# Gated mix of a long convolution and an MLP: the convolution by halves of 1024, three spectral products per frequency, the sums on POOL

## The chip, the core and the metric

The kernel runs on one core of one Trainium2 chip. The core has TensorE (PE in the profile; PEld is its weight load), VectorE (DVE), ScalarE (ACT), GpSimd (POOL) and SyncE (SP, which here only issues DMAs). The metric is the device time of one execution in microseconds (us).

## What is computed

The inputs are q, k, v and x = q of shape (1, 2048, 512), short and long convolution kernels per channel, and the two weights of an MLP of width 1792.

```python
x = A_q
g = sigmoid((x * gate_w).sum(-1, keepdims=True))
# a: short causal convolution of k (4 taps), times v, then a causal convolution of
#    length 2048 with ssm_k per channel (by FFT of 4096), plus kv * ssm_D, times q
kv = k_shift * v
y = irfft(rfft(kv, 4096) * rfft(ssm_k, 4096))[:2048] + kv * ssm_D
a = q * y
b = relu(x @ w1) @ w2
out = g * a + (1 - g) * b
```

All of it is float32. The kernel adds ssm_D to the first tap of ssm_k, so that the second term of y needs no work of its own.

## The kernel before

Two streams of work share the engines. The MLP has 4 chunks of 512 tokens and 14 slices of the hidden width. To keep float32 accuracy, each operand is split into a high and a low part (`parted`, `relu`, `rest`), and each product is three matmuls of 128x128 by 128x512: lines L314 to L316 for the first layer, L341 to L343 for the second, 1344 matmuls in all. ACT makes the high part of the hidden layer (hh, L326) and DVE the low part (hl, L329).

The long convolution is a Fourier transform written as small matmuls in float32, each of which PE runs as two passes. It works in three stages, with DRAM tensors `sa` and `sb` between them for the transposes:

- Stage one (`conv_h`, `conv_x`, `stage1`): for each of 8 pieces c, the long kernel (h) and the product kv (x, made by DVE from four taps, L432 to L448) are multiplied by a 64x128 matrix of complex exponentials (L380). Four matmuls of 64 rows by 128 columns fill four PSUM banks; ACT copies them out (L386) and SP stores them to `sa`.
- Stage two (`conv_mid`): for each of 8 groups g, the second transform of h and of x (`rounds`, L476: eight tiles of 64x32 per round, two rounds each), the complex product of both spectra on ACT and DVE (copies L490 and L493, eight products L506, four sums L513), and the first inverse transform (`inverse`, L524: 16 tiles of 32x64 in two rounds), copied out by ACT and DVE (L533, L535) and stored to `sb`.
- Stage three (`conv_end`): for each pair of 16 token blocks, the last transform (L586, four matmuls of 128x64), then the gate, the product with q (L595) and the sum with the MLP's result (L548). The MLP's result of the first 12 blocks waits in the DRAM tensor `bd` (L353, L599).

The kernel issues nothing in program order. Every operation is given to a planner (`Plan.add`) with an engine, a planned duration, a rank, what it depends on, and what it takes and gives of the buffers in `room` ("cv" are four of the eight PSUM banks; the other four hold the second layer's sums). `Plan.order` steps through time with these planned durations and writes down a fixed order for each engine; on the chip each engine runs that order and waits on semaphores where data or buffers aren't there. So the order on every engine is fixed beforehand, and bursts of small tiles (`tiles=True`) stand between runs of MLP matmuls. All loads and stores go through SP's queue, except two small constants that POOL loads.

Of the kernel before, what the change touches and what calls it, by code (L numbers as in the profile page):

```python
# [18 lines left out]


# [5 lines left out]
def _w(e):  # L26
    return np.exp(-2j * np.pi * (np.asarray(e) % (4 * S)) / (4 * S))
# [13 lines left out]
def _constants():  # L41

    n1, k1 = np.arange(64)[:, None], np.arange(64)[None]
    w = _w((4 * k1 + 1) * 32 * n1)
    s1 = np.stack([w.real, w.imag], -1).reshape(64, 128)
    s1 = np.concatenate([s1, s1], 0)

    fw = np.zeros((2, 2, 32, NJ, 2, 32))  # L50
    iv = np.zeros((4, 32, 8, 2, 2, 2, 32))
    n2, k2 = np.arange(32)[:, None], np.arange(32)[None]
    for j in range(NJ):
        for b in range(2):
            k1 = 2 * j + b
            c = _w((4 * k1 + 1 + 256 * k2) * n2)
            fw[b, 0, :, j, 0] = c.real
            fw[b, 1, :, j, 0] = -c.imag
            fw[b, 0, :, j, 1] = c.imag
            fw[b, 1, :, j, 1] = c.real  # L60
            c = np.conj(c.T)
            iv[j % 4, :, j // 4, 0, b, 0] = c.real
            iv[j % 4, :, j // 4, 1, b, 0] = -c.imag
            iv[j % 4, :, j // 4, 0, b, 1] = c.imag
            iv[j % 4, :, j // 4, 1, b, 1] = c.real
    cc = np.concatenate([fw.reshape(P, 8, 2 * P), iv.reshape(P, 8, 2 * P)], 2)


    c = np.conj(_w((4 * np.arange(64)[:, None] + 1) * 32 * np.arange(64)[None])) / S
    ib = np.stack([c.real, -c.imag], 1).reshape(P, 64)  # L70
    return s1, cc, ib
# [7 lines left out]
class Plan:  # L79
# [19 lines left out]
    def order(self):  # L99
# [14 lines left out]
        while True:  # L114
            for eng, ops in ready.items():
# [4 lines left out]
                if eng == "PE" and any(o["rank"][0] == 1 and not o["take"] for o in ops):  # L120
                    held = {t for o in ops + soon if o["rank"][0] == 0 and len(o["take"]) > 1 for t in o["take"]}
# [83 lines left out]
def build(tc, wf, xp, qn, kn, vn, hn, dn, sh, gw, w1, w2, cs1, ccc, cib, out):  # L205
# [11 lines left out]
    sa = dram.tile([2, P, 32, D], F32, name="sa")  # L217
    sb = dram.tile([P, 32, D], F32, name="sb")
# [3 lines left out]
            "cc": 2, "acc": ACC, "tmp": TMP, "ev": EV, "r": RB, "ha": HAB, "p": PB, "bv": BVB,  # L222
# [151 lines left out]
    def stage1(t, c, key, rank, after, give):  # L374
        def go():
            for r in range(R):
                z = slice(r * D, (r + 1) * D)
                for half in range(2):
                    at = slice(64 * half, 64 * half + 64)
                    mm(bank(("s1" + t, c, half, r)), T["s1t",][at, :], T[key][at, z], start=True, stop=True)  # L380

        m = add("PE", R * TILES, (0, rank), go, [after, s1ld], ["cv"] * 2 * R, give, tiles=True)
        for r in range(R):
            for half in range(2):
                def out_(r=r, half=half):
                    nc.scalar.copy(tile_of(("ev" + t, c, half, r), "ev"), T["s1" + t, c, half, r])  # L386

                def put(r=r, half=half):
                    queue[QUEUE["s1"]].dma_start(sa["hx".index(t), :, 16 * half + R * c + r], T["ev" + t, c, half, r])

                v = add("ACT", act_time(D, True), (0, *rank), out_, [m], ["ev"], ["cv"])
                stores.append(add(QUEUE["s1"], ISSUE[QUEUE["s1"]], (-5000, *rank), put, [v], (), ["ev"], dma=ROW))
# [63 lines left out]
    def conv_mid(g, gate):  # L456
# [4 lines left out]
        def load(t, u):  # L461
            def ld():
                tile_of(k("r", t, u), "r", 2 * D)
                for i in range(2):
                    j = 4 * g + 2 * u + i
                    nc.sync.dma_start(T[k("r", t, u)][:, i * D:(i + 1) * D], sa["hx".index(t), 4 * j:4 * j + 4].rearrange("k n d -> (k n) d"))
# [3 lines left out]
        def rounds(t, os):  # L470
            for o in os:
                ps = [bank(k("f", t, o, b)) for b in range(2)]
                for j in range(4):
                    for b in range(2):
                        at = slice(64 * b, 64 * b + 64)
                        mm(ps[b][32 * j:32 * j + 32, :], T[k("cc")][at, 64 * j + 32 * o:64 * j + 32 * o + 32],  # L476
                           T[k("r", t, j // 2)][at, (j % 2) * D:(j % 2 + 1) * D], start=True, stop=True)
# [5 lines left out]
        ha = {}  # L483
        for o in range(2):
            if o % HS == 0:
                fh = add("PE", HS * TILES, (0, rank), lambda o=o: rounds("h", range(o, o + HS)), h + [cc], ["cv"] * 2 * HS + ["ha"] * 2 * HS,
                         ["r"] * 2 if o + HS == 2 else (), fifo=["f"], tiles=True)
            for b in range(2):
                if b or not HD:
                    ha[o, b] = add("ACT", act_time(D, True), rank, lambda o=o, b=b: nc.scalar.copy(tile_of(k("ha", o, b), "ha"), T[k("f", "h", o, b)]),  # L490
                                   [fh], (), ["cv"], fifo=["ha"])
                else:
                    ha[o, b] = add("DVE", dve_time(D), (0, rank), lambda o=o, b=b: nc.vector.tensor_copy(tile_of(k("ha", o, b), "ha"), T[k("f", "h", o, b)]),  # L493
                                   [fh], (), ["cv"], fifo=["ha"])
        d = dve_time(D)
        prev, y = {}, {}
        for o in range(2):
            if o % XS == 0:
                fx = add("PE", XS * TILES, (0, rank), lambda o=o: rounds("x", range(o, o + XS)), x + [cc], ["cv"] * 2 * XS + ([] if o else ["p"] * 4),
                         ["r"] * 2 if o + XS == 2 else (), fifo=["f"], tiles=True)  # L500
            for b in range(2):
                for i in range(2):

                    def mul(o=o, b=b, i=i):
                        src = T[k("ha", i ^ o, b)]
                        tt(src if o else tile_of(k("p", i, b), "p"), T[k("f", "x", o, b)], src, op=OP.mult)  # L506

                    prev[o, b, i] = add("DVE", d, rank, mul, [fx, ha[i ^ o, b], prev.get((0, b, 0)), prev.get((0, b, 1))] if o else [fx, ha[i, b]],
                                        (), ["cv"] if i else (), fifo=() if o else ["p"])
                if o:  # L510
                    for i in range(2):
                        def join(b=b, i=i):
                            tt(T[k("p", i, b)], T[k("p", i, b)], T[k("ha", 1 - i, b)], op=OP.add if i else OP.subtract)  # L513

                        y[i, b] = add("DVE", d, rank, join, [prev[0, b, i], prev[1, b, i], prev[1, b, 1]], (), ["ha"])

        def inverse():
            ps = [bank(k("iv", j)) for j in range(4)]
            for o in range(2):
                for b in range(2):  # L520
                    for j in range(4):
                        at = slice(32 * j, 32 * j + 32)
                        c = 2 * P + P * o + 64 * b
                        mm(ps[j][64 * b:64 * b + 64, :], T[k("cc")][at, c:c + 64], T[k("p", o, b)][at, :], start=o == 0, stop=o == 1)  # L524

        iv = add("PE", 2 * TILES, (0, rank), inverse, list(y.values()), ["cv"] * 4, ["p"] * 4 + ["cc"], tiles=True)
        for j in range(4):
            def put(j=j):
                m = 4 * (4 * g + j)
                queue[QUEUE["iv"]].dma_start(sb[m:m + 4].rearrange("k n d -> (k n) d"), T[k("bv", j)])  # L530

            if j % 2 or not VD:
                bv = add("ACT", act_time(D, True), rank, lambda j=j: nc.scalar.copy(tile_of(k("bv", j), "bv"), T[k("iv", j)]), [iv], ["bv"], ["cv"])  # L533
            else:
                bv = add("DVE", dve_time(D), (0, rank), lambda j=j: nc.vector.tensor_copy(tile_of(k("bv", j), "bv"), T[k("iv", j)]), [iv], ["bv"], ["cv"])  # L535
# [21 lines left out]
    def conv_end(n, gate):  # L557
# [5 lines left out]
        def ld():  # L563
            nc.sync.dma_start(rows(tile_of(k("br"), "br", 2 * D)), sb[:, n::16])
# [17 lines left out]
        def go():  # L582
            for u in (n - 1, n):
                ps = bank(("y", u))
                for i in range(2):
                    mm(ps[64 * i:64 * i + 64, :], T["ibt",], T["br", u][:, i * D:(i + 1) * D], start=True, stop=True)  # L586
# [150 lines left out]
```

## Time and profile before

| | |
|---|---|
| runs, median (lowest to highest) | 426.07 us (425.86 to 427.87) |
| profiled execution, its own time | 426.14 us |
| its span in the trace | 424.4 us |
| busy: PE, DVE, ACT, POOL | 416.2, 256.4, 120.3, 1.4 us |
| moved by DMA | 94.09 MB, mean 222 GB/s |
| granted TensorE clock | 0.999 of full speed |

The span is what the trace covers; the time of an execution contains a little around it. Busy times are sums over the span, and an average over stages with different limits. Stage one runs to about 156 us of the span, stage two from 170 to 319 us, stage three from 338 to 401 us; MLP matmuls stand between all bursts and end the kernel.

### The profile page before, as it was taken

How to read it: one execution, taken by the hardware profiler on the slowest of the kernel's cores; microseconds unless marked ns; L12 is line 12 of the kernel's file. 1: busy time of each engine (PE TensorE's matmuls, PEld its weight loads, DVE VectorE, ACT ScalarE, POOL GpSimd, SP SyncE). 2: the span in 40 equal slices, each digit the busy share in tenths (PEclk: the TensorE clock that was granted, in tenths of full speed). 3: DMA queues.
4: the chain of work that ended last, by engine and by line, in shares of the span. 5: the costliest groups of instructions: out<-in, count | busy, mean ns of one | idle time of the engine just before them, and what ended most of it. 6: DMA issues, size and time to landing. Idle time of an engine off the chain costs nothing.

```text
span 424.4 us, 6184 instructions
## 1 busy us (share of the span) xinstructions
PE 416.2 (98%) x2317; PEld 277.5 (65%) x2317; DVE 256.4 (60%) x394; ACT 120.3 (28%) x227; POOL 1.4 (0%) x6
## 2 busy tenths in 40 slices
PE   8999999999999999999999999999999999999994
PEld 7676767767767768555565655556577676776583
DVE  4599999979746101658584656748572356456412
ACT  4536454426433331121431112121132410111010
POOL 0000000000000000000000000000000000000000
PEclk9999999999999999999999999999999999999999
DMA  8998896978965448446886544645207898888002
GB/s 267 332 349 299 299 332 228 352 254 271 321 217 191 163 180 265 163 148 221 276 274 194 191 153 166 228 151 174 99 2 230 284 322 284 291 288 278 36 0 99
DMA packets 47503, 94.09 MB, mean 222 GB/s; under 512 B 5073, under 2 KB 5841, under 8 KB 47346
## 3 DMA queue, kind: packets, MB, share of 16 engines
q1 hardware_dynamic: 47410, 93.61, 65.0%
q8 instruction: 18, 0.29, 0.3%
q0 software_dynamic: 64, 0.10, 0.1%
q14 instruction: 11, 0.09, 0.1%
HBM read 61.18 MB, written 32.51 MB: 221 GB/s over the span
## 4 chain that ended last, share of the span: by engine, by line
PE 96%; DMA 2%; DVE 1%; issue 1%; ACT 0%; DVEq 0%; ACTq 0%
PE m L341 13%; PE m L314 12%; PE m L343 12%; PE m L315 12%; PE m L316 12%; PE m L342 12%; PE f_h L476 4%; PE iv L524 4%; PE f_x L476 4%; PE y L586 4%; PE s1h L380 3%; PE s1x L380 3%; PE m L298 2%; DMA sa<-ev 1%; PE warm L610 1%
## 5 line engine op out<-in xcount | busy, mean ns | idle before, releaser
L341 PE MATMUL m<-w1h_h,hh 128*128 128x512 f32 x224 | 92.0, 411 | 0.9 <-ACT hh L326 0.9
L343 PE MATMUL m<-w1h_h,hl 128*128 128x512 f32 x224 | 87.6, 391 | 0.1
L329 DVE SCALAR_TENSOR_TENSOR hl<-m,hh 128x512 fp32r<-128x512 f32 x56 | 38.5, 689 | 81.4 <-ACT hh L326 81.2
L342 PE MATMUL m<-w1l_l,hh 128*128 128x512 f32 x224 | 87.5, 391 | 0.0
L314 PE MATMUL m<-xh_h,w0h_h 128*128 128x512 f32 x192 | 76.6, 399 | 0.2 <-ACT ev L386 0.2
L326 ACT ACTIVATE hh<-m 128x512 fp32r<-128x512 f32 x56 | 33.4, 598 | 151.8 <-PE m L316 151.3
L315 PE MATMUL m<-xl_l,w0h_h 128*128 128x512 f32 x192 | 75.0, 390 | 0.0
L316 PE MATMUL m<-xh_h,w0l_l 128*128 128x512 f32 x192 | 74.8, 390 | 0.0
L341 PEld LDWEIGHTS m<-w1h_h,hh 128*128 128x128 f32 x224 | 42.0, 187 | 40.2 <-issue 28.9
L314 PEld LDWEIGHTS m<-xh_h,w0h_h 128*128 128x128 f32 x192 | 36.0, 188 | 19.9 <-issue 10.8
L343 PEld LDWEIGHTS m<-w1h_h,hl 128*128 128x128 f32 x224 | 42.1, 188 | 10.1 <-DVE hl L329 1.0
L342 PEld LDWEIGHTS m<-w1l_l,hh 128*128 128x128 f32 x224 | 42.1, 188 | 7.3
L316 PEld LDWEIGHTS m<-xh_h,w0l_l 128*128 128x128 f32 x192 | 36.1, 188 | 7.8
L315 PEld LDWEIGHTS m<-xl_l,w0h_h 128*128 128x128 f32 x192 | 36.1, 188 | 7.1
L438 DVE TENSOR_TENSOR acc<-acc,tmp 128x1024 f32<-128x1024 f32 x24 | 29.4, 1224 | 0.7
L506 DVE TENSOR_TENSOR p<-f_x,ha 128x512 f32<-128x512 f32 x32 | 19.9, 682 | 10.9 <-PE f_x L476 10.9
L535 DVE COPY bv<-iv 128x512 f32<-128x512 f32 x16 | 10.3, 686 | 21.8 <-PE iv L524 21.8
L386 ACT COPY ev<-s1x 128x512 f32<-128x512 f32 x32 | 16.8, 599 | 18.2 <-PE s1x L380 10.0
L386 ACT COPY ev<-s1h 128x512 f32<-128x512 f32 x32 | 16.8, 598 | 15.8 <-PE s1h L380 13.4
L435 DVE TENSOR_TENSOR tmp<-in,sht_sht 128x512 f32<-128x512 f32 x32 | 21.3, 682 | 0.0
L513 DVE TENSOR_TENSOR p<-p,ha 128x512 f32<-128x512 f32 x32 | 20.7, 681 | 0.0
L506 DVE TENSOR_TENSOR ha<-f_x,ha 128x512 f32<-128x512 f32 x32 | 19.8, 678 | 0.0
(59 smaller groups left out, 354.3 us busy)
## 6 DMA issues: line engine op xcount, KB each, us to landing
sa<-ev SPq DMA_DIRECT2D x64, 256.0 KB, 3.6
r_h<-sa SPq DMA_DIRECT2D x32, 256.0 KB, 3.8
r_x<-sa SPq DMA_DIRECT2D x32, 256.0 KB, 4.6
sb<-bv SPq DMA_DIRECT2D x32, 256.0 KB, 3.3
br<-sb SPq DMA_DIRECT2D x16, 512.0 KB, 5.3
raw<-w SPq DMA_DIRECT2D x26, 256.0 KB, 4.8
in<-kn SPq DMA_DIRECT2D x10, 512.0 KB, 6.0
raw<-xp SPq DMA_DIRECT2D x16, 256.0 KB, 3.9
```

The source lines that it names most:

```text
L314: mm(ps, part("h", f, k), T["x", "h", c, k], start=k == 0, stop=False)
L315: mm(ps, part("h", f, k), T["x", "l", c, k], start=False, stop=False)
L316: mm(ps, part("l", f, k), T["x", "h", c, k], start=False, stop=k == 3)
L326: nc.scalar.activation(tile_of(("hh", c, f), "hh", dt=F32R, p=mp, bufs=HHB), T["m1", c, f], AF.Relu)
L329: nc.vector.scalar_tensor_tensor(tile_of(("hl", c, f), "hl", dt=F32R, p=mp, bufs=HHB), T["m1", c, f], 0.0, T["hh", c, f].bitcast(F32), op0 ...
L341: mm(ps, T["hh", c, f][:, z], T["w", "h", 1, f], start=f == 0, stop=False)
L342: mm(ps, T["hh", c, f][:, z], T["w", "l", 1, f], start=False, stop=False)
L343: mm(ps, T["hl", c, f][:, z], T["w", "h", 1, f], start=False, stop=f == NF - 1)
L386: nc.scalar.copy(tile_of(("ev" + t, c, half, r), "ev"), T["s1" + t, c, half, r])
L438: nc.vector.tensor_tensor(T["acc", c], T["acc", c], T[dst], op=OP.add)
L476: mm(ps[b][32 * j:32 * j + 32, :], T[k("cc")][at, 64 * j + 32 * o:64 * j + 32 * o + 32], T[k("r", t, j // 2)][at, (j % 2) * D:(j % 2 + 1) ...
L506: tt(src if o else tile_of(k("p", i, b), "p"), T[k("f", "x", o, b)], src, op=OP.mult)
```

## The change

The convolution is cut into halves of 1024 tokens, h0 and h1 of the kernel and x0 and x1 of the input. The first output half needs h0 * x0, the second h1 * x0 + h0 * x1. Transforms then have length 1024 with the same number of points in total, and at each frequency there are three complex products instead of two. The matrix of stage one becomes 32x64 and that of stage three 64x32.

Stage one: eight tiles in one burst instead of four.

```diff
-            for r in range(R):
-                z = slice(r * D, (r + 1) * D)
-                for half in range(2):
-                    at = slice(64 * half, 64 * half + 64)
-                    mm(bank(("s1" + t, c, half, r)), T["s1t",][at, :], T[key][at, z], start=True, stop=True)
+            ps = [bank(("s1" + t, c, i)) for i in range(4)]
+            for r in range(R):
+                for i in range(4):
+                    at = slice(32 * i, 32 * i + 32)
+                    mm(ps[i][64 * r:64 * r + 64, :], T["s1t",][at, :], T[key][at, r * D:(r + 1) * D], start=True, stop=True)
```

Stage three: eight tiles instead of four.

```diff
-            for u in (n - 1, n):
-                ps = bank(("y", u))
-                for i in range(2):
-                    mm(ps[64 * i:64 * i + 64, :], T["ibt",], T["br", u][:, i * D:(i + 1) * D], start=True, stop=True)
+            ps = [bank(("y", u)) for u in (n - 1, n)]
+            for u in range(4):
+                for b in range(2):
+                    at = slice(64 * b, 64 * b + 64)
+                    mm(ps[b][32 * u:32 * u + 32, :], T["ibt",][at, :], T["br", n - 1 + u // 2][at, (u % 2) * D:(u % 2 + 1) * D], start=True, stop=True)
```

Stage two keeps the tiles of `rounds` and `inverse`. Bank 0 of a round now holds the first half and bank 1 the second, and o is the real or imaginary part. With hz = H0, gz = H1 (into which DVE takes H0 as it reads H1 from PSUM: H1's real part less H0's imaginary part, H1's imaginary part plus H0's real part), the products and sums are:

```diff
+            fh.append(copy(hz[o], k("f", "h", o, 0), [m], ["cv"]))
+        fg = [dve(gz[o], k("f", "h", o, 1), hz[1 - o], OP.add if o else OP.subtract, [m, fh[1 - o]], ["cv"], rank=(0, rank)) for o in range(2)]
+        for s, w, f in ((0, hz, fh), (1, gz, fg)):
+            for o in range(2):
+                prev = last[s, o] = dve(pz[s][o], k("f", "x", 0, 0), w[o], OP.mult, [fx, f[o], prev], ["cv"] if s and o else ())
+        e = copy(k("x1", 0), k("f", "x", 0, 1), [fx], ["cv"], "xs")
+        u0 = dve(k("u", 0), k("x1", 0), hz[0], OP.mult, [e], (), "u", ["u"])
+        u1 = dve(k("x1", 0), k("x1", 0), hz[1], OP.mult, [u0])
+        last[1, 0] = both(ADD[0], pz[1][0], pz[1][0], k("u", 0), OP.add, [last[1, 0], u0], ["u"])
+        last[1, 1] = both(ADD[0], pz[1][1], pz[1][1], k("x1", 0), OP.add, [last[1, 1], u1], ["xs"])
+        us = [dve(k("v", o), k("f", "x", 1, 0), hz[1 - o], OP.mult, [fx, last[0, o]], (), "u", ["u"]) for o in range(2)]
+        ug = [dve(gz[1 - o], k("f", "x", 1, 0), gz[1 - o], OP.mult, [fx, last[1, o], *us], ["cv"] if o else ()) for o in range(2)]
+        e = copy(k("x1", 1), k("f", "x", 1, 1), [fx], ["cv"], "xs")
+        uh = [dve(hz[1 - o], k("x1", 1), hz[1 - o], OP.mult, [e, us[o], u0, u1], ["xs"] if o else ()) for o in range(2)]
+        for o in range(2):
+            last[0, o] = both(ADD[1], pz[0][o], pz[0][o], k("v", o), sub[o], [last[0, o], us[o]], ["u"])
+        for o in range(2):
+            last[1, o] = both(ADD[2], pz[1][o], pz[1][o], gz[1 - o], sub[o], [last[1, o], ug[o]], ["z"])
+        for o in range(2):
+            last[1, o] = both(ADD[3], pz[1][o], pz[1][o], hz[1 - o], sub[o], [last[1, o], uh[o]], ["z"])
```

`dve` is a DVE tensor_tensor, `copy` an ACT copy out of PSUM, and `both` issues a tensor_tensor on the engine that it is given: with ADD = ['POOL', 'POOL', 'POOL', 'POOL'] all eight sums of a group run on POOL, planned at POOLT = 1.37 us each. The tensors hz, gz and p take 12 buffers "z" (8 per group), u and v two buffers "u", and the copies of x1 one buffer "xs".

The constants, DRAM layouts and planner settings:

```diff
-        cc = add("SP", ISSUE["SP"], rank[1] - 0.5, lambda: nc.sync.dma_start(tile_of(k("cc"), "cc", 4 * P), ccc[:, g]),
-                 [gate], ["cc"], dma=ROW, fifo=["cc"])
+        cw = add("SP", ISSUE["SP"], rank[1] - 0.5, lambda: nc.sync.dma_start(tile_of(k("cw"), "cw", 2 * P), ccc[:, g, :2 * P]),
+                 [gate], ["cw"], dma=ROW // 2, fifo=["cw"])
+        ci = add("SP", ISSUE["SP"], rank[1] + 1.2, lambda: nc.sync.dma_start(tile_of(k("ci"), "ci", P), ccc[:, g, 2 * P:]),
+                 [gate], ["ci"], dma=ROW // 4, fifo=["ci"])
-            nc.sync.dma_start(rows(tile_of(k("br"), "br", 2 * D)), sb[:, n::16])
+            nc.sync.dma_start(rows(tile_of(k("br"), "br", 2 * D)), sb.rearrange("b k n d -> (b k) n d")[:, 2 * n:2 * n + 2])
-SAFE = dict(PE0=1.0, PE1=0.175, ACT=0, DVE=0.4)
+SAFE = dict(PE0=0.6, PE1=0.175, ACT=0, DVE=0.4)
-HHB = 3
-M2R = 2.5
+HHB = 2
+M2R = 1.5
-X0 = -32.0
-XP = 21.0
+X0 = -25.0
+XP = 24.0
-W0 = -80
+W0 = -90
```

The fixed orders that come out of it, for groups 2 to 6 of stage two (names of the diff; the group is in brackets, "hl" is an MLP instruction):

```
PE before:  iv[g-1], 6 MLP, x (two rounds)[g], 12 to 18 MLP, h [g+1], 6 to 9 MLP, h [g+1], 15 to 36 MLP
PE after:   iv[g-1], 6 MLP, h (two rounds)[g+1], 6 MLP, x [g+1], 6 MLP, x [g+1], 30 MLP
DVE after:  gz1, gz0, p00, u0, p01, u1, hl, p10, v0, p11, v1, gz1*x, hl, gz0*x, hz1*x1, hz0*x1, bv, bv
POOL after: p10+u0, p00-v0, p11+u1, p01+v1, p10-gz1*x, p11+gz0*x, p10-hz1*x1, p11+hz0*x1
```

The H tensors of group g+1 take the four buffers that the H tensors of group g held: its hz copies on ACT wait for the fifth and sixth sum of group g, its gz instructions on DVE for the seventh and eighth. In all, before the last burst of stage three stand 1335 MLP matmuls after and 1269 before; 9 and 75 follow it.

More of the change, by code (lines that the diff above doesn't have):

```diff
@@ L18 @@
 NJ = 32
+H = S // 2
 def _w(e):
[L27 removed]
+    return np.exp(-2j * np.pi * (np.asarray(e) % (4 * H)) / (4 * H))
 def _round12(x):
@@ L120, in order @@
                 if eng == "PE" and any(o["rank"][0] == 1 and not o["take"] for o in ops):
-                    held = {t for o in ops + soon if o["rank"][0] == 0 and len(o["take"]) > 1 for t in o["take"]}
+                    held = {"cv" for o in ops + (soon if SOON else []) if o["tiles"] and len(o["take"]) >= HOLD and all(self.turn[q][0] == o["n"] for q in o["fifo"])
+                            and all(t == "cv" or self.room[t] >= o["take"].count(t) for t in o["take"])}
                 for op in ops:
@@ L479, in conv_mid, with rounds @@
-        cc = add("SP", ISSUE["SP"], rank[1] - 0.5, lambda: nc.sync.dma_start(tile_of(k("cc"), "cc", 4 * P), ccc[:, g]),
-                 [gate], ["cc"], dma=ROW, fifo=["cc"])
+        def rounds(t, o):
+            ps = [bank(k("f", t, o, b)) for b in range(2)]
+            for j in range(4):
+                for b in range(2):
+                    at = slice(64 * b, 64 * b + 64)
+                    mm(ps[b][32 * j:32 * j + 32, :], T[k("cw")][at, 64 * j + 32 * o:64 * j + 32 * o + 32],
+                       T[k("r", t, j // 2)][at, (j % 2) * D:(j % 2 + 1) * D], start=True, stop=True)
@@ new lines, in conv_mid, with both, go @@
+        a, d = act_time(D, True), dve_time(D)
+        z = lambda *nm: tile_of(k(*nm), "z")
+        def both(eng, dst, x, y, op, deps, give=(), new=None, take=(), rank=rank):
+            def go():
+                if new:
+                    tile_of(dst, new)
+                (nc.vector if eng == "DVE" else nc.gpsimd).tensor_tensor(T[dst], T[x], T[y], op=op)
+            return add(eng, d if eng == "DVE" else POOLT, rank, go, deps, take, give, fifo=[new] if new else ())
+        dve = lambda *a, **kw: both("DVE", *a, **kw)
@@ new lines, in conv_mid, with copy, go, forward_h @@
+        gps = lambda *a, **kw: both("POOL", *a, **kw)
+        def copy(dst, src, deps, give, new=None):
+            def go():
+                nc.scalar.copy(tile_of(dst, new) if new else T[dst], T[src])
+            return add("ACT", a, rank, go, deps, [new] if new else (), give, fifo=[new] if new else ())
+        hz, gz, pz = [k("h0", o) for o in range(2)], [k("g", o) for o in range(2)], [[k("p", s, o) for o in range(2)] for s in range(2)]
+        def forward_h(o):
+            tile_of(hz[o], "z")
+            tile_of(gz[o], "z")
+            rounds("h", o)
@@ new lines, in forward_x @@
+        def forward_x(o):
+            if o == 0:
+                for key in pz[0] + pz[1]:
+                    tile_of(key, "z")
+            rounds("x", o)
+        fh = []
+        for o in range(2):
+            m = add("PE", TILES, (0, 1, rank[1] + RK["H"]), lambda o=o: forward_h(o), h + [cw], ["cv"] * 2 + ["z"] * 2, ["r"] * 2 if o else (), fifo=["f"], tiles=True)
+            fh.append(copy(hz[o], k("f", "h", o, 0), [m], ["cv"]))
+        fg = [dve(gz[o], k("f", "h", o, 1), hz[1 - o], OP.add if o else OP.subtract, [m, fh[1 - o]], ["cv"], rank=(0, rank)) for o in range(2)]
@@ L715 @@
         "xp": xT,
-        "qn": halves(q),
+        "qn": tokens(q),
         "kn": kn,
```

147 lines of the change are left out of this document (59 added, 88 removed).

## The prediction

> **What bounds the kernel now.** I read the page first: the share of each engine and the chain of work that ended last.
>
> ```profile
> span 424.4 us, 6184 instructions
> ...
> PE 416.2 (98%) x2317; PEld 277.5 (65%) x2317; DVE 256.4 (60%) x394; ACT 120.3 (28%) x227; POOL 1.4 (0%) x6
> ...
> PE 96%; DMA 2%; DVE 1%; issue 1%; ACT 0%; DVEq 0%; ACTq 0%
> ```
>
> PE is busy for 98% of the span and holds 96% of the chain, while POOL is empty. A busy PE need not be an efficient one, so the next view is what PE waited for.
>
> ```profile
> PE warm L610 <- DVE zero_zero L605: 1.2, 1, 1.2
> PE m L341 <- ACT hh L326: 0.9, 1, 0.9
> PE m L314 <- ACT ev L386: 0.2, 1, 0.2
> ```
>
> That is the whole list, 2.3 us. PE is fed throughout: what is taken off PE comes off the end, and a wait put into PE's fixed order is added to it. The third view is the chain in order of time, for what PE pays for each burst of small tiles (columns: start, length, what; a plain matmul of 128x512 between others takes 0.23).
>
> ```profile
> 34.40 1.92 PE s1x L380 x8
> 36.32 0.43 PE m L341
> ...
> 170.07 1.02 PE f_h L476 x16
> 171.09 0.43 PE m L314
> ...
> 187.37 1.90 PE iv L524 x32
> 189.27 0.43 PE m L341
> 190.63 0.24 PE m L343
> 190.86 1.88 PE f_x L476 x32
> ...
> 317.04 1.90 PE iv L524 x32
> ...
> 337.70 1.87 PE y L586 x8
> 339.56 0.43 PE m L314
> ```
>
> A record counts two passes for one float32 matmul: x16 are the eight tiles of one round. One round that fills the array costs 1.02 (f_h). The iv burst, 16 tiles of 32x64 in two rounds, costs 1.90. The first and last stages pay two rounds (1.92, 1.87) for only four matmuls, since 64x128 and 128x64 tiles fit the array two at a time. The first plain matmul after a burst takes 0.43 instead of 0.23, so each burst carries 0.20 more.
>
> **The change, part by part.** *First stage.* Each of the 16 bursts becomes eight 32x64 tiles in one round. No row shows exactly eight such tiles alone. Half of iv's burst, 0.95, bounds the round from below, and 1.92 bounds it from above if the tiles didn't run side by side. I take f_h's 1.02, the nearest (eight tiles, one round, float32). It saves 1.92 - 1.02 = 0.90 per burst, 14.4 us in 16. *Last stage.* Eight bursts become eight 64x32 tiles, which is the shape of f_h: 1.87 - 1.02 = 0.85, 6.8 us in all. *Middle on PE.* The rounds of a group stay: two for h, two for x, two for iv. Before, a group issues two single h bursts and one joined x burst (2 x 1.22 + 2.08 with their restarts); after, the issue order has one joined h burst and two single x bursts in groups 2 to 7, two joined ones in group 0 and four single ones in group 1. The total is the same: 0. The number of MLP matmuls (1344) stays too.
>
> *What the products cost.* DVE has 16 instructions per group on both sides: two copies, eight products, four sums and two evictions become two differences against PSUM, twelve products and two evictions. ACT gets two copies more per group, 16 in all. The sums, eight per group, go to POOL. The prices:
>
> ```profile
> L506 DVE TENSOR_TENSOR p<-f_x,ha 128x512 f32<-128x512 f32 x32 | 19.9, 682 | 10.9 <-PE f_x L476 10.9
> L513 DVE TENSOR_TENSOR p<-p,ha 128x512 f32<-128x512 f32 x32 | 20.7, 681 | 0.0
> L329 DVE SCALAR_TENSOR_TENSOR hl<-m,hh 128x512 fp32r<-128x512 f32 x56 | 38.5, 689 | 81.4 <-ACT hh L326 81.2
> L438 DVE TENSOR_TENSOR acc<-acc,tmp 128x1024 f32<-128x1024 f32 x24 | 29.4, 1224 | 0.7
> L490 ACT COPY ha<-f_h 128x512 f32<-128x512 f32 x16 | 9.4, 585 | 31.5 <-PE f_h L476 31.5
> L730 POOL MEMSET const-float32-0.0<- 128x1 f32 x1 | 0.1, 99 | 0.2 <-issue 0.2
> ```
>
> POOL's only compute row, 99 ns for one element, says nothing of a sum, so I bound it by DVE's rows. From 512 to 1024 elements DVE goes from 0.681 to 1.224: 0.138 fixed and 0.543 per pass of 512. One pass is the lower end, 0.68 (POOL as fast as DVE). Three passes, both operands and the result one after another, are the upper end: 0.138 + 3 x 0.543 = 1.77. I take two passes, 1.22, the row of 1024 elements. The change gives its planner 1.37 for a sum, and PE's order was laid out for that.
>
> *Where a late sum reaches PE.* Call the price P. In the new order, PE issues per group (2 to 6) iv, 6 MLP matmuls, the joined h burst, 6, x burst, 6, x burst, 30. MLP pitch, from 24 matmuls in a row:
>
> ```profile
> 410.36 0.39 PE L341 MATMUL m<-w1h_h,hh 128*128 128x512 f32 x1
> ...
> 415.80 0.39 PE L341 MATMUL m<-w1h_h,hh 128*128 128x512 f32 x1
> ```
>
> (415.80 - 410.36) / 24 = 0.227. So a group takes 48 x 0.227 + 2.10 + 2.08 + 2 x 1.22 = 17.5 us of PE. A handoff between engines is about 0.1: the last iv burst ends at 317.04 + 1.90 = 318.94, and DVE starts on it at 319.00.
>
> ```profile
> 319.00 1.29 DVE L535 COPY bv<-iv 128x512 f32<-128x512 f32 x2 [2.04 <-PE iv L524]
> ```
>
> Two loops lead through POOL. Loop A: the new group's fourth H tensor takes the buffer that POOL's eighth sum of the old group reads, and DVE writes it just ahead of the new group's first product. From that product, six DVE instructions (five of this group and one hl, 4.1), handoff, eight sums, handoff, one DVE instruction 0.68: A = 5.0 + 8P. Loop B: the second x burst's second bank is copied by ACT only after POOL's third sum has freed the one buffer xs, and the old group's iv needs that bank: 4.1 + 3P + 0.59 + iv 2.10 + 6 MLP 1.36 + h 2.08 + 6 MLP 1.36 + x 1.02 and handoffs 0.3: B = 12.9 + 3P. At P = 1.22, A is 14.8 and B 16.6, at 1.37 they are 16.0 and 17.0, all under 17.5: no wait, cost 0. The limits are 1.56 for A and 1.53 for B. The cover is thus PE's own 17.5 us; past the limits all that stands behind DVE's waiting H tensor (the products, the hl that the MLP needs) holds PE, for some six groups. At 1.77, A is 19.2, which costs 1.7 x 6 = 10.
>
> The Trainium skill (GPSIMD Engine Reference, section "Performance versus the Vector engine") has the same add at 2048 float32 in 4497 ns on GpSimd against 2293 on DVE; by that ratio, 1.96, an estimate of a sum is 1.33, and the total below would not change. No run here shows it yet.
>
> *DMA and SP.* The constants come as 128 and 64 KB instead of 256 KB per group, one issue more per group on SP; the loads that they stand among are issued well ahead. In the first stage PE reaches the fourth x burst with two more weight steps done (48 matmuls, four tiles of 256 KB, 1.05 MB), while the stage's inputs stay:
>
> ```profile
> 60.00:80.00 20.00, 19.98 (x86) 13.91 (x85) 19.83 (x26) 9.29 (x18) 0.00 (x0) 1.00 0.81 274
> ...
> 340.00:360.00 20.00, 20.00 (x86) 13.79 (x86) 12.10 (x26) 2.60 (x7) 0.00 (x0) 1.00 0.89 302
> 360.00:380.00 20.00, 20.00 (x87) 13.83 (x86) 11.54 (x25) 2.38 (x7) 0.00 (x0) 1.00 0.88 287
> ```
>
> With a DMA share of 0.81 there is room; the bounds are 0 and 1.05 MB / 0.3 = 3.5 us, and I take 1.0. DVE, 19.83 of 20 busy there, does the same work on both sides; by the counts, the tenth hl of the first chunk stands 3 us earlier on PE with 1 us less of DVE work ahead of it. It had 9 us to spare: 0.
>
> *Last stage's transfers.* Each y burst takes 1.05 MB of br and 0.52 each of q, b (first six bursts) and out.
>
> ```profile
> br<-sb SPq DMA_DIRECT2D x16, 512.0 KB, 5.3
> q<-qn SPq DMA_DIRECT2D x16, 256.0 KB, 4.8
> ...
> 324.28 0.63 SPq L564 DMA_DIRECT2D br<-sb  x1
> ```
>
> The first br is issued 5.3 us after iv's end. The sixth y burst now stands 237 MLP matmuls and five bursts behind iv, 59.8 us, or 54.5 after that issue. Up to it 6 x (1.05 + 0.52 + 0.52) + 5 x 0.52 = 15.1 MB must pass, at 295 GB/s (the two stretches above) 51.3 us, and 3.5 to land (5.3 less its own 1.8): 54.8. It is late by 0.3, or by 2 if the rate were the second stretch's: I take 0.5.
>
> *Tail.* Only 9 MLP matmuls (2.0 us) follow the last y burst, where 75 did.
>
> ```profile
> L548 DVE SCALAR_TENSOR_TENSOR o<-m,gs,t 128x512 f32<-128x512 f32 x3 | 2.2, 750 | 6.3 <-PE m L343 4.7 <-DMA out<-o 1.5
> ...
> 417.46 2.05 DMA out<-o
> ...
> 420.30 0.48 DVE o L548
> ...
> 418.30 0.39 PE L343 MATMUL m<-w1h_h,hl 128*128 128x512 f32 x1
> ```
>
> After it DVE has two t and two o (0.75 each) and two halves (0.48); the last o waits for the store of the one two before it (2.05 and its issue). From the burst's end that is about 5.0 us, 2.8 after PE's end, against (420.30 + 0.48) - (418.30 + 0.39) = 2.1 before: +0.7.
>
> **Sum.** Against the profiled execution's own time, 426.14 (span 424.4 and 1.7 around it; the runs' median is 426.07): 426.14 - 14.4 - 6.8 + 0.0 + 1.0 + 0.5 + 0.7 = 407.1. I forecast 407.
>
> **The rivals.** *1, sums late, gain partly lost.* A POOL sum takes 1.6 to 1.95 us, or the two engines hold each other up. For it: no row shows POOL at work beside DVE. Two of DVE's products per group (x1 by H, the last two) read both operands from SBUF while POOL runs; if each held POOL for its 0.68, loop A grows by 1.36. With P = 1.37 that is 17.4, still nothing; with 1.77 it is 20.5, 3.0 x 6 = 18: 425. Without it, 417. Time 411 to 425, middle 417. Against it: the layout leaves 0.15 to 0.3 us per sum. The Trainium skill (SBUF — State Buffer, "Who interferes with whom") has a rule that speaks for this rival: a DVE instruction with two SBUF inputs contends with a GpSimd instruction that reads SBUF, and the second one issued blocks until the first is done. L513 is such an instruction, but POOL stood idle beside it, so no run here shows the rule yet.
>
> *2, slower: POOL becomes the bound of the middle.* The place is loop A, the price 8P per group, and it decides from (17.5 + 19.0 / 6 - 5.0) / 8 = 1.96 us, where the 19 us are gone (1.79 with the two held products). At three whole DVE instructions per sum, 2.04, A is 21.3: 3.8 x 6 = 23, time 430. For it: POOL's speed is unknown and nothing else fills PE when DVE stands. Against it: that price lies above my upper end.
>
> *3, the last stage is bound by transfers.* Bursts of y come every 8.4 us instead of 8.8 and need 2.6 MB each, 8.8 us at 295. If the store queue slows the loads behind it, 2 to 5 us: 411. Against it: the last two bursts need no b.
>
> *4, the small tiles don't run side by side in the first stage* (the change doesn't do what it says): 14.4 comes back, 421. Against it: iv does so in the rows above.
>
> **How the numbers follow.** Chances: forecast (403 to 410) 0.59, rival 1 0.20, rival 2 0.12, rival 3 0.06, rival 4 0.03. About 0.5%, 2.1 us, is what a measurement can tell from no change. Rival 1's top end gives "same" 0.03; slower is rival 2, 0.12; faster is the rest, 0.85. The range goes from 403 (the sum without its three additions, 404.9, and without the 2.3 us that PE waits now, rounded) to 425 (POOL's upper end, with DVE and POOL holding each other up).
>
> **What would show it.** After the change: s1 and y bursts of 1.0 in the chain (wrong: 1.9); POOL busy 64 x P, with P between 0.7 and 1.5 (rival 1 or 2: more); PE's wait list still free of waits on POOL, or on DVE's H tensors or ACT's xs copy (else loops A or B); iv bursts 17.5 us apart; DVE's rows for x1 by H at 0.68 (longer: contention); y bursts without a DMA wait. A PE share under 96%, or a middle longer than 150 us, would make the prediction wrong.

## The result and the profile after

| | before | after |
|---|---|---|
| runs, median (lowest to highest) | 426.13 us (425.86 to 427.87) | 1000.87 us (998.92 to 1001.71) |
| ratio, with its 95% interval | | 2.346 (2.339 to 2.353) |
| span of the profiled execution | 424.4 us | 999.7 us |

The change more than doubles the time; 407 was forecast. The page of the changed kernel, the lines that answer to those of before:

```profile
span 999.7 us, 6664 instructions
...
PE 577.5 (58%) x2509; PEld 317.2 (32%) x2509; DVE 272.2 (27%) x394; ACT 131.7 (13%) x243; POOL 89.5 (9%) x70
...
DMA packets 44369, 93.53 MB, mean 94 GB/s; under 512 B 2961, under 2 KB 5793, under 8 KB 44210
...
q1 hardware_dynamic: 44274, 93.07, 26.1%
...
DMA 60%; PE 20%; SPq 15%; DVE 2%; issue 1%; ACT 1%; DVEq 0%; ACTq 0%
DMA sa<-ev 25%; DMA r_x<-sa 13%; SPq L469 12%; DMA r_h<-sa 9%; DMA raw<-w 5%; DMA sb<-bv 4%; DMA bd<-o 3%; PE m L316 3%; PE m L317 3%; PE m L318 3%; PE f_x L478 2%; PE m L343 2%; PE m L345 2%; PE m L344 2%; SPq L392 2%
```

PE has gone from 96% of the chain to 20%. POOL, the new element, is busy for 9%. What holds the chain is DMA, and in it the transfers to and from `sa` and SP's queue standing at their issue (SPq). The bytes are nearly the same as before (93.5 against 94.1 MB); the rate fell from 222 to 94 GB/s. The list of waits agrees (us in total, times, longest):

```profile
ACT ev L388 <- DMA sa<-ev: 193.5, 40, 9.6
...
PE f_h L478 <- DMA r_h<-sa: 93.0, 22, 18.4
...
PE f_x L478 <- DMA r_x<-sa: 71.6, 22, 4.6
```

The transfers of `sa` in the changed kernel (duration of the issue on SP in ns, min/median/max, then first and last start) and two stretches of it by windows (the stretch and its length, the busy us of PE, PEld, DVE, ACT and POOL, the granted TensorE clock, the busy share of the 16 DMA engines, GB/s):

```profile
L392 SPq DMA_DIRECT2D sa<-ev x64: 485/4948/6523, 21.7 to 389.8; - x64
L469 SPq DMA_DIRECT2D r_h<-sa x32: 507/4944/5473, 408.6 to 815.6; - x32
L469 SPq DMA_DIRECT2D r_x<-sa x32: 941/4996/5473, 418.8 to 836.4; - x32
```

```profile
350.00:375.00 25.00, 15.84 (x60) 6.88 (x60) 0.00 (x0) 2.93 (x5) 0.00 (x0) 0.69 0.13 51
375.00:400.00 25.00, 15.42 (x52) 11.42 (x50) 1.98 (x3) 3.34 (x6) 0.00 (x0) 0.80 0.13 52
```

SP stands for 4.95 us at an issue (the median of the 64), 256 KB each time: 53 GB/s. And the DMA share is 0.13, which is what 2 fully busy engines of 16 give; 16 engines that idle most of the time would give it too, which the experiments below decide. The same view of the kernel before (the last line is who waited for these transfers: us, times):

```profile
L389 SPq DMA_DIRECT2D sa<-ev x64: 319/327/1655, 22.0 to 157.5; - x64
L466 SPq DMA_DIRECT2D r_h<-sa x32: 320/422/1420, 159.5 to 279.3; - x32
...
  ACT ev L386: 6.2, 3
```

There an issue takes a third of a microsecond, and the 64 stores pass in 136 us instead of 368.

Three lines of the change, which neither the diff above nor the prediction shows, give the reason to suspect. They are the transfers whose DRAM side became two blocks of 64 rows:

```diff
-                    ...dma_start(sa["hx".index(t), :, 16 * half + R * c + r], T["ev" + t, c, half, r])
+                ...dma_start(sa["hx".index(t), i % 2, :, n:n + R].rearrange("k n d -> n k d"), T["ev" + t, c, i])
-                    ...dma_start(T[k("r", t, u)][:, i * D:(i + 1) * D], sa["hx".index(t), 4 * j:4 * j + 4].rearrange("k n d -> (k n) d"))
+                    ...dma_start(T[k("r", t, u)][:, i * D:(i + 1) * D], sa["hx".index(t), :, 2 * j:2 * j + 2].rearrange("b r n d -> b (r n) d"))
-                ...dma_start(sb[m:m + 4].rearrange("k n d -> (k n) d"), T[k("bv", j)])
+                ...dma_start(sb[:, m:m + 2].rearrange("b r n d -> b (r n) d"), T[k("bv", j)])
```

Before, the outermost dimension of all three is 128 rows; after, it is 2. 64 stores to `sa`, 64 loads from it and 32 stores to `sb` are 160 transfers; at 4.95 us each, one after another, that is an estimate of 792 us. The Trainium skill (DMA: Bandwidth & Descriptors, section "Why a DMA increments its semaphore by 16 and not by 1") has a rule for it: a DMA is spread over the largest number of engines up to 16 that divides the size of each side's outermost dimension. By that rule these transfers run on 2, and the trace agrees, with a share of 0.13 where 2 of 16 would be 0.125.

### The profile page after: what moved, and what is told of

It is laid out like the page before. It is cut to its first block, busy times and chain, and to the rows that moved or that the text cites. A ratio compares the mean times of both kernels' runs of the same rounds, so it can differ in the third digit from the quotient of the medians.

```text
span 999.7 us, 6664 instructions
## 1 busy us (share of the span) xinstructions
PE 577.5 (58%) x2509; PEld 317.2 (32%) x2509; DVE 272.2 (27%) x394; ACT 131.7 (13%) x243; POOL 89.5 (9%) x70
## 2 busy tenths in 40 slices
DMA packets 44369, 93.53 MB, mean 94 GB/s; under 512 B 2961, under 2 KB 5793, under 8 KB 44210
## 4 chain that ended last, share of the span: by engine, by line
DMA 60%; PE 20%; SPq 15%; DVE 2%; issue 1%; ACT 1%; DVEq 0%; ACTq 0%
DMA sa<-ev 25%; DMA r_x<-sa 13%; SPq L469 12%; DMA r_h<-sa 9%; DMA raw<-w 5%; DMA sb<-bv 4%; DMA bd<-o 3%; PE m L316 3%; PE m L317 3%; PE m L318 3%; PE f_x L478 2%; PE m L343 2%; PE m L345 2%; PE m L344 2%; SPq L392 2%
## 5 line engine op out<-in xcount | busy, mean ns | idle before, releaser
L343 PE MATMUL m<-w1h_h,hh 128*128 128x512 f32 x224 | 104.6, 467 | 79.6 <-ACT hh L328 50.0
L478 PE MATMUL f_h<-r_h,cw 64*32 64x512 f32 x256 | 64.9, 984 | 129.8 <-DMA r_h<-sa 93.0
L316 PE MATMUL m<-xh_h,w0h_h 128*128 128x512 f32 x192 | 91.8, 478 | 48.6 <-ACT ev L388 37.9
L345 PE MATMUL m<-w1h_h,hl 128*128 128x512 f32 x224 | 97.8, 437 | 10.9 <-DVE hl L331 10.9
L494 POOL TENSOR_TENSOR z<-z,u 128x512 f32<-128x512 f32 x24 | 31.5, 1328 | 765.8 <-DVE u L494 485.2
L478 PE MATMUL f_x<-r_x,cw 64*32 64x512 f32 x256 | 55.1, 775 | 71.6 <-DMA r_x<-sa 71.6
L317 PE MATMUL m<-xl_l,w0h_h 128*128 128x512 f32 x192 | 85.6, 446 | 0.0
L383 PE MATMUL s1x<-acc,s1c_s1t 32*64 32x512 f32 x128 | 34.5, 908 | 56.3 <-DVE hl L331 29.6
L494 DVE TENSOR_TENSOR z<-f_x,z 128x512 f32<-128x512 f32 x48 | 32.5, 682 | 122.2 <-PE f_x L478 122.2
L494 DVE TENSOR_TENSOR z<-f_h,z 128x512 f32<-128x512 f32 x16 | 10.3, 688 | 184.9 <-PE f_h L478 184.9
L494 POOL TENSOR_TENSOR z<-z,z 128x512 f32<-128x512 f32 x32 | 46.8, 1487 | 20.3 <-DVE z L494 20.3
```

The source lines that it names most:

```text
L316: mm(ps, part("h", f, k), T["x", "h", c, k], start=k == 0, stop=False)
L317: mm(ps, part("h", f, k), T["x", "l", c, k], start=False, stop=False)
L343: mm(ps, T["hh", c, f][:, z], T["w", "h", 1, f], start=f == 0, stop=False)
L345: mm(ps, T["hl", c, f][:, z], T["w", "h", 1, f], start=False, stop=f == NF - 1)
L383: mm(ps[i][64 * r:64 * r + 64, :], T["s1t",][at, :], T[key][at, r * D:(r + 1) * D], start=True, stop=True)
L478: mm(ps[b][32 * j:32 * j + 32, :], T[k("cw")][at, 64 * j + 32 * o:64 * j + 32 * o + 32], T[k("r", t, j // 2)][at, (j % 2) * D:(j % 2 + 1) ...
```

## The experiments

The theory: a transfer uses as many DMA engines as its outermost dimension counts, here 2. The rivals: the scatter of rows over DRAM costs; SP's standing issue is the limit; or the new order on PE and POOL costs. The first four kernels split transfers into halves of 64 rows each, so that the outermost dimension is 64, and leave all else. Where neither a range nor a ratio is given, the time of a changed kernel is that of one execution.

**All three groups split.**

```diff
-                ...dma_start(sa["hx".index(t), i % 2, :, n:n + R].rearrange("k n d -> n k d"), T["ev" + t, c, i])
+                for r in range(R):
+                    ...dma_start(sa["hx".index(t), i % 2, :, n + r], T["ev" + t, c, i][64 * r:64 * r + 64, :])
...
+                    for b in range(2):
+                        ...dma_start(T[k("r", t, u)][64 * b:64 * b + 64, i * D:(i + 1) * D], sa["hx".index(t), b, 2 * j:2 * j + 2].rearrange("r n d -> (r n) d"))
...
+                for b in range(2):
+                    ...dma_start(sb[b, m:m + 2].rearrange("r n d -> (r n) d"), T[k("bv", j)][64 * b:64 * b + 64, :])
```

> The changed kernel with each store of stage one, each load of r and each store to sb issued as two DMAs of 64 rows instead of one DMA whose DRAM side is two blocks of 64 rows; same bytes, same rows, same order of everything else, 160 issues more on SP. Theory (a DMA whose DRAM side has an outermost dimension of 2 runs on 2 of the 16 DMA engines): the DMA share of 0.13 goes, transfers land in 3 to 6 us, and the time is what was forecast for the changed kernel, 405 to 420 us. Rival (the strided rows themselves are slow, or POOL's sums are): the same rows stay slow, above 900 us.

**One group split at a time**: the stores of stage one, the loads of the middle, the stores of the middle.

> Only the 64 stores of stage one split in two. Theory: stage one falls from 408 to about 165 us, the rest stays: 740 to 780 us. Rival (loads and stores share one cause elsewhere): no change, 1000 us.

> Only the 64 loads of r split in two. Theory: 64 x 5.0 = 320 us of queue go, the 32 stores to sb (160 us) stay hidden beside PE's 140 us or bind the middle at about 180: 690 to 760 us. Rival: no change.

> Only the 32 stores to sb split in two. Theory: 32 x 5.0 = 160 us of queue go: 830 to 860 us. Rival: no change.

| split | time, us | against 1000.87 |
|---|---|---|
| all three | 422.67 (420.73 to 423.71) | -578 |
| stores to `sa` | 762.26 | -239 |
| loads from `sa` | 755.32 | -246 |
| stores to `sb` | 889.60 | -111 |

The three parts add up to 595, nearly the whole 578: each kind costs by itself, in series. Cut into halves, the transfers take back all of the loss, with the order on PE, ACT, DVE and POOL unchanged. The last one missed its expectation: with 32 transfers instead of 64 it gives 111, or 3.5 us per transfer. The full version stands at 0.991 (0.987 to 0.994) of before. It lies just above the 420 that was expected of it, and 15 us above the forecast; that rest has its own experiments below.

**The rule without the change.** In the kernel before, only the order in which the 64 stores write their 128 rows is altered (and the constant's columns with it), so that the outermost dimension is OUT = 2, 4 or 8. The rows written are the same.

```diff
-                    ...dma_start(sa["hx".index(t), :, 16 * half + R * c + r], T["ev" + t, c, half, r])
+                    ...dma_start(sa["hx".index(t), :, 16 * half + R * c + r].rearrange("(a o) d -> o a d", o=OUT), T["ev" + t, c, half, r])
```

> The kernel before, with nothing of the change in it; only its 64 stores of stage one write the same 128 rows of 2 KB in another order, so that the outermost dimension of their DRAM side is 2 (the constant's columns are permuted to match; the result is the same). Theory (a transfer is spread over as many DMA engines as its outermost dimension counts, here 2): each store takes 256 KB in 4.9 to 5.0 us, the 64 of them 317 us in a row as after the change, where stage one took about 165; the time is 630 to 690. Rival (it is the changed kernel's scatter of rows over DRAM, or its order on PE and POOL, that costs): 424 to 432, since the rows written are the same.

> The same as b2 with an outermost dimension of 4. Theory: 256 KB in about 2.5 us, 64 stores in 160 us, about as long as stage one lasts: 428 to 480. Rival of the scatter: the same time as b2, whatever that is.

> The same as b2 with an outermost dimension of 8. Theory: 256 KB in about 1.3 to 2 us, 64 stores in under 130 us and hidden: 425 to 435. Rival of the scatter: the same time as b2.

Measured: 667.33, 515.49 and 443.32 us, against 426.35 with all 128 rows outermost. The rival of the scatter falls, since the rows are the same in all three. Two of the expectations were too low. The number of engines can also be counted. The pages' lines on packets, in order the kernel before and those with 2, 4 and 8 outermost:

```profile
DMA packets 47503, 94.09 MB, mean 222 GB/s; under 512 B 5073, under 2 KB 5841, under 8 KB 47346
DMA packets 46607, 94.09 MB, mean 141 GB/s; under 512 B 4177, under 2 KB 4945, under 8 KB 46450
DMA packets 46735, 94.09 MB, mean 183 GB/s; under 512 B 4305, under 2 KB 5073, under 8 KB 46578
DMA packets 46991, 94.09 MB, mean 213 GB/s; under 512 B 4561, under 2 KB 5329, under 8 KB 46834
```

The bytes stay, and the packets under 512 B become fewer by 896, 768 and 512. For 64 stores that is 14, 12 and 8 each, just as if a store had one small packet for every engine that it uses: 16 before, then 2, 4 and 8. The changed kernel and the version with all three groups split fit too: 2961 and 7761 packets under 512 B, 4800 more, which is 160 x (2 x 16 - 2). So the transfers ran on two engines, not slowly on 16. The stores' issues on SP with 2 outermost:

```profile
L391 SPq DMA_DIRECT2D sa<-ev x64: 485/4820/5622, 22.0 to 387.6; - x64
```

With 4, the same view, and behind it the windows over the time of these stores:

```profile
L391 SPq DMA_DIRECT2D sa<-ev x64: 508/517/2054, 22.2 to 244.7; - x64
```

```profile
0.00:245.00 245.00, 197.01 (x680) 128.87 (x681) 113.72 (x142) 70.35 (x128) 0.87 (x5) 0.86 0.51 173
```

With 8, and who waited for the stores:

```profile
L391 SPq DMA_DIRECT2D sa<-ev x64: 576/580/2044, 21.7 to 177.5; - x64
...
  ACT ev L388: 40.3, 26
```

With 4 engines the stores last 222 us where I had counted 160. The four engines also carry their sixteenth of everything else: 245 us at 173 GB/s are 42.4 MB, of which the stores are 16.8, so each engine has 25.6 / 16 = 1.6 MB more. At 53 / 2 = 26.5 GB/s per engine that gives 16.8 / 4 / 26.5 = 158 us and another 60: about 218. The same sum gives 317 + 60 = 377 us for 2 engines, where 366 was measured. For 8 it gives 139, less than the 156 that the stores last; the kernel still loses 17 us. ACT waits for single stores (40.3 us in 26 waits, against 6.2 in 3 before), and PE's waits, 2.3 us in all before, come to 13.4; what the remaining 6 us are was not traced.

**Two queues.** In the changed kernel every second store of stage one goes to ACT's queue (the planner lays out the engines' orders anew with it).

```diff
-                queue[QUEUE["s1"]].dma_start(...)
+                queue[("SP", "ACT")[i % 2]].dma_start(...)
```

> The changed kernel with every second store of stage one issued on ACT's queue instead of SP's; the access patterns stay. In the changed kernel SP itself stands 5 us at each such issue (a median of 4948 ns where before 327). Theory (the two DMA engines are the limit, and the transfers of both queues fall on the same two): the last store is issued near 390 us as in the changed kernel, ACT's issues block for about as long as SP's, the time is 960 to 1020. Rival (the blocked issue on one queue is the limit, or each queue gets a pair of engines of its own): the stores pass twice as fast, the last one is issued by about 240 us, and the time is 830 to 880.

Measured: 992.96 us. The stores' issues:

```profile
L392 SPq DMA_DIRECT2D sa<-ev x32: 485/491/837, 19.8 to 393.1; - x32
L392 ACTq DMA_DIRECT2D sa<-ev x32: 485/500/3997, 39.1 to 393.6; - x32
```

Now hardly a store's issue stands (medians 0.49 and 0.50 us), and the last store still starts at 393 us, as with one queue (389.8). The standing issue is a consequence; the two engines are the limit. With a pair of engines for each queue the stores would have passed sooner, so both queues' transfers share the same two.

**A layout with 64 or more rows outermost.** `sa` and `sb` are laid out as half, n, k. A store to `sa` becomes one contiguous block, a load from it and a store to `sb` have 64 pieces outermost, and only the loads of the last stage are cut in two. The constants' rows and columns are exchanged to match.

```diff
-    sa = dram.tile([2, 2, 64, 32, D], F32, name="sa")
+    sa = dram.tile([2, 2, 32, 64, D], F32, name="sa")
...
+                ...dma_start(sa["hx".index(t), i % 2, n:n + R].rearrange("n k d -> (n k) d"), T["ev" + t, c, i])
...
+                    ...dma_start(T[k("r", t, u)][:, i * D:(i + 1) * D], sa["hx".index(t), :, :, 2 * j:2 * j + 2].rearrange("b n r d -> (b n) r d"))
```

> The changed kernel with the two arrays in DRAM laid out anew: sa as half, n, k and sb as half, n, k. The stores of stage one become one contiguous block, the loads of the middle and its stores have 64 pieces outermost, and only the 16 loads of the last stage become two transfers each: 16 transfers more than before the change, where the version with all three groups split has 160 more. Theory A (what is left between that version's 422.7 and the forecast's 407 is mostly the load of 160 more issues on SP and the smaller transfers): 407 to 415. Theory B (it is mostly the new order on PE, ACT and POOL: bank waits of 0.3 to 0.5 us per group in the middle, one POOL chain, waits in the first stage): 417 to 423. Under both the new transfers of 256 KB take 1.5 to 3 us where they took 4.95, and the time is below 426.

> As f1_layout in stage one and the loads of the middle; sb keeps the changed kernel's layout with its store split in two halves of 64 rows, so that the last stage's loads are one contiguous transfer of 512 KB with 4 KB pieces again (32 transfers more in the middle, 16 fewer at the end). In f1_layout the first y burst waited for q and br (two pieces of 7.5 and 10.0 us on DMA in the chain, a DMA share of 0.98 to 1.04 at 272 to 281 GB/s). Theory (2 KB pieces of br cost the last stage 4 to 5 us): 406 to 411. Rival (the last stage has to move the same bytes, whatever the pieces): 412 to 415.

Measured: 412.81 us, ratio 0.967 (0.963 to 0.970), and 412.44 us, ratio 0.966 (0.963 to 0.968). Both beat both kernels. Against the version with 160 transfers more this is 10 us, so theory A of the first expectation holds for two thirds of the 15 us (transfers of half the size, twice the issues; the two weren't told apart). The second expectation's theory falls: larger pieces in the last stage bring 0.4 us, inside the spread. The line numbers of these versions are one or two higher. The waits of PE in the second one, all of them:

```profile
PE m L317 <- ACT ev L389: 2.6, 3, 1.2
PE warm L646 <- DVE zero_zero L641: 1.2, 1, 1.2
PE m L344 <- ACT hh L329: 1.1, 1, 1.1
PE f_h L479 <- DVE hl L332: 0.6, 1, 0.6
PE m L346 <- DVE hl L332: 0.6, 2, 0.4
PE m L317 <- ACT z L504: 0.2, 1, 0.2
```

Its chain of work in order of time (start, length, what):

```profile
127.28 1.04 PE s1x L384 x16
...
136.84 1.16 PE s1h L384 x16
...
138.60 4.10 DMA sa<-ev
...
239.68 1.90 PE iv L558 x32
...
243.17 1.88 PE f_h L479 x32
...
257.46 1.90 PE iv L558 x32
...
401.55 1.02 PE y L622 x16
```

Two iv bursts of the chain of the kernel before, again with 48 MLP matmuls between them:

```profile
263.96 1.90 PE iv L524 x32
...
281.58 1.90 PE iv L524 x32
```

Windows of the first 400 us, of this version and of the kernel before (behind the stretch and its length, 400.00, comes PE busy):

```profile
0.00:400.00 400.00, 393.63 (x2478) 264.26 (x2479) 267.69 (x387) 130.93 (x243) 90.85 (x70) 1.00 0.71 231
```

```profile
0.00:400.00 400.00, 397.52 (x2238) 263.29 (x2240) 250.34 (x385) 119.13 (x225) 1.40 (x6) 1.00 0.69 233
```

PE's waits have neither POOL nor a DMA among the names. What the forecast missed by is spread out: PE is idle for 6.4 us of these 400 where it was 2.5 before, and iv bursts are 17.78 apart where they were 17.62.

**More sums.** The same kernel with four sums more per group on POOL (the last two sums of a group are taken back and done again).

> f2_layout_sb with four sums more per group on POOL at the end of its chain (the last sums are taken back and done again, so the result stays but for rounding). The prediction's loop A, 5.0 + 8P, stands at 5.0 + 8 x 1.41 = 16.3 us with the measured mean of a sum, 1.5 under the group's 17.8 on PE. Theory (loop A as priced): 5.6 us more per group, of which 1.5 are hidden: 4.1 x 6 = 25 us over f2_layout_sb, 425 to 440, with waits on POOL or on DVE's H tensors in PE's list. Rival (POOL has more slack than that): within 5 us of f2_layout_sb.

Measured: 428.87 us, 16.4 more than without the extra sums; the theory had priced 25. Windows over three groups, first of the kernel without and then of the one with the extra sums (the column after ACT is POOL):

```profile
239.68:293.01 53.33, 53.33 (x440) 30.19 (x443) 38.89 (x55) 13.88 (x24) 32.73 (x25) 1.00 0.65 186
```

```profile
242.31:304.75 62.44, 55.61 (x433) 30.59 (x432) 38.60 (x55) 13.87 (x24) 48.11 (x37) 1.00 0.56 160
```

PE's waits that are new with the extra sums:

```profile
PE f_x L479 <- DVE z L495: 7.6, 6, 1.3
PE m L317 <- DVE hl L332: 5.4, 6, 1.0
```

Per group, POOL is busy 10.9 us in the first and 16.0 in the second, and the pitch is 17.78 and 20.81. In the second the loop is the bound: 20.81 - 16.0 = 4.8 lie outside POOL, where the prediction had 5.0. In the first the loop is then 4.8 + 10.9 = 15.7, so 2.1 us of the 5.1 added are hidden and 3.0 are paid per group (the expectation had 5.6 added, 1.5 hidden and 4.1 paid). The waits are where the prediction put them: PE behind DVE's z and behind hl.

**The sums on DVE.** `ADD = ['DVE', 'DVE', 'DVE', 'DVE']` in the same kernel.

> f2_layout_sb with all eight sums of a group on DVE instead of POOL (the planner orders the rest anew). DVE gets 8 x 0.68 = 5.4 us more per group and is rid of the two products of 1.38 that take 0.68 without POOL beside them: about 12.9 + 5.4 - 1.4 = 16.9 us of the group's 17.8. Theory (POOL's place pays little here, since PE is the bound either way): within 4 us of f2_layout_sb. Rival (without POOL, DVE holds PE in the middle): 8 to 25 us more than f2_layout_sb.

Measured: 424.31 us (423.48 to 424.97), ratio 0.994 (0.992 to 0.996), 12 us more than with POOL. The rival holds. PE's longest waits:

```profile
PE m L317 <- DVE hl L332: 6.0, 5, 1.4
PE y L622 <- DMA br<-sb: 5.9, 2, 5.6
```

Two iv bursts of its chain:

```profile
249.29 1.90 PE iv L558 x32
...
268.30 1.90 PE iv L558 x32
```

The pitch is 19.0, and the MLP waits for hl, which stands behind the sums on DVE. Another 5.9 us are waits for `br` in the last stage, in an order that the planner made anew; whether the sums or this order cause them stays open.

## Why the prediction was wrong

The step that failed is "DMA and SP". It priced the change's DMAs by bytes and by the number of issues: "one issue more per group", 1.05 MB more in stage one, the rate of the last stage. It added 1.0 us, and took it that the loads "are issued well ahead". The stores and loads of `sa` and the stores of `sb` keep their bytes and their count, so they got no price at all, and none of the four rivals contains them. They changed their shape: 128 rows outermost became 2. In that place the runs showed 160 transfers one after another on two engines each, 792 us by the estimate above; cut into halves of 64 rows, they took 578 us off the time. What happened resembles rival 2 only in its sign; in the changed kernel POOL was busy for 9% and bounded nothing.

The other steps can be read in the second layout version, where no transfer has 2 outermost any more (412.44 against 407.0):

- *First and last stage on PE.* Right. Bursts of s1 are 1.04 and of y 1.02 in the chain: 16 x 0.88 + 8 x 0.85 = 20.9 saved, where 21.2 was forecast. Rival 4 is out.
- *Price of a sum.* POOL is busy for 89.5 us in the changed kernel, 1.4 of it without the sums: 1.38 for each of the 64, where 1.22 was taken and the bounds were 0.68 and 1.77. The estimate by the Trainium skill (GPSIMD Engine Reference, section "Performance versus the Vector engine"), 1.33, was nearer.
- *Contention, rival 1.* It is there, and it stays inside loop A's 2.1 us to spare. The median sum of z and u takes 1.30 us. The sums of z and z stand partly beside DVE's last two products of x1, which read two SBUF operands: 1.66, and up to 1.74. Those two products take 1.46 (median), and 0.68 with the sums on DVE. In the second layout version (ns, min/median/max):

```profile
L495 POOL TENSOR_TENSOR z<-z,z x32: 1268/1664/1744, 182.9 to 317.6; 128x512 f32<-128x512 f32 x32
L495 POOL TENSOR_TENSOR z<-z,u x24: 1277/1296/1745, 177.5 to 310.0; 128x512 f32<-128x512 f32 x24
...
L495 DVE TENSOR_TENSOR z<-xs,z x16: 678/1464/1772, 188.0 to 314.8; 128x512 f32<-128x512 f32 x16
```

- *Loops A and B.* Loop A was right: its constant is 4.8 against 5.0, it is hidden with 2.1 us to spare, and in the run with more sums it costs 3.0 per group. Loop B never showed as a wait of PE.
- *Middle on PE*, forecast as 0: the group that was summed to 17.5 us took 17.62 before and 17.78 after. The prediction's sum starts from the kernel before, so the difference counts: 0.16, some 1.0 us over six groups.
- *DMA in stage one and the last stage*, 1.5 forecast: PE's idle time up to 400 us grew by 3.9, mostly waits for ACT's ev (2.6 against 0.2), one of them behind a store that ACT waited for (4.10 in the chain above). So 2.4 us of the miss are here.
- *Tail*, 0.7 forecast. PE's last matmul ends at 404.85 of 410.7 us, so 5.9 us follow it; before, 5.7 did (418.69 of 424.4). The tail costs 0.1, 0.6 less than forecast:

```profile
404.45 0.40 PE L346 MATMUL m<-w1h_h,hl 128*128 128x512 f32 x1
```

Of the 5.4 us of the miss these steps give 0.3 + 1.0 + 2.4 - 0.6 = 3.1; some 2.3 stay unexplained.

## What to carry to other kernels

When a change alters the layout of a DRAM tensor, write down the outermost dimension of both sides of every DMA that touches it, before and after; equal bytes and an equal number of issues did not keep its time here. In a profile, the sign was a DMA share that sits at a few sixteenths (0.13). A queue that stands at its issues came with it at 2 engines, but not at 4, where the median issue took 0.52 us. The cure was an outermost dimension of 64 or 128, by another layout or by cutting the transfer; another queue wasn't. Work put on an empty engine pays only up to the loop that leads through it, and here that loop could be summed from the rows before the change (5.0 beside the sums, 4.8 measured).

## What the hardware showed that I had not expected

- An issue on SP, 0.33 us before, stood for 4.95 us when its transfers had only two engines, and with it the queue that carries all other loads. With half of the stores on ACT's queue the issues took 0.5 us, and the stores passed no sooner. The Trainium skill (DMA: Bandwidth & Descriptors, section "Issuing engines are not separate DMA queues") says that the engines are shared by all queues; the trace agrees (last store at 393.6 us with two queues, 389.8 with one).
- With 2, 4 and 8 engines for the same rows the time was 667, 515 and 443 us; an estimate from 53 GB/s on two engines is 26.5 GB/s for each. Even 8 of 16 cost 17 us.
- Where PE stood waiting, the granted clock was lower: 0.69 and 0.80 in the two stretches above, against 0.999 over the kernel before. One f_h matmul took 984 ns on average instead of 601. The busy time of all of them rose further, from 17.4 to 64.9 us, and that isn't the clock alone: a burst also came in pieces of a few matmuls, each behind its own transfer (the third line). The f_h rows of the kernel before and of the changed one (busy us, mean ns), and such a piece:

```profile
L476 PE MATMUL f_h<-r_h,cc 64*32 64x512 f32 x256 | 17.4, 601 | 0.0
L478 PE MATMUL f_h<-r_h,cw 64*32 64x512 f32 x256 | 64.9, 984 | 129.8 <-DMA r_h<-sa 93.0
427.24 1.92 PE L478 MATMUL f_h<-r_h,cw 64*32 64x512 f32 x4 [3.21 <-DMA r_h<-sa]
```
